# The first strip's last two groups by seven products, with the weight sums kept in the activations' places

## The chip, the cores and the metric

The program runs on one core of one Trainium2 chip. The metric is the time of one execution on the device in microseconds, measured several times; shown are the median and the extremes. The profile comes from a further execution under the hardware profiler. In its lines PE is TensorE, DVE is VectorE, ACT is ScalarE, POOL is GpSimd and SP is the engine that issues the transfers; L264 is line 264 of the kernel.

## The reference

```python
def _attn_ref(q, k, v, g_norm):                      # 8 batches, 8 heads, 576 tokens, 64 features
    kv = np.einsum('bhsd,bhse->bhde', k, v)
    out = np.einsum('bhsd,bhde->bhse', q, kv)
    rms = np.sqrt(np.mean(out * out, axis=-1, keepdims=True) + 1e-06)
    return (out / rms * g_norm).astype(np.float32)

def _moe_ref(x, w_in, w_out):                        # 4608 tokens, d_model 512, d_ff 2048
    h = x @ w_in
    r = np.maximum(h, 0.0)
    return (r * r @ w_out).astype(np.float32)
```

Linear attention without a mask, a norm per head, and a feed-forward block with squared Relu. Everything is in float32, but the two weight matrices come as 64-bit floats.

## The kernel before, in words

**Strips.** The 4608 tokens go in nine strips of 512. For each, `X @ W_in` (the first product, "up"), the squared Relu and the second product ("down") with `W_out` follow each other. Attention for the next strips is cut into slices that are put between the steps of a strip.

**Seven products for eight.** A matrix product whose operands are cut in four blocks can be made from seven block products and some sums (Strassen's scheme in Winograd's form). The kernel does so almost everywhere. For up, a group `g` (four in all) holds 256 features of each half of d_ff. `w_in` has its four blocks a11, a21, a12, a22 and `w_s` the three sums s1 = a21 + a22, s2 = s1 - a11 and s4 = a12 - s2; the last difference, a11 - a21, is written over a21. X needs four such sums too, t1 to t4. `up(s, g, p)` makes product p of a group in the order 1, 2, 6, 5, 7, 3, 4, with four matrix instructions of 128x256 each. Products 1, 6, 7 and 4 add up in one bank of PSUM ("ps_A"), 5 and 3 in another ("ps_B"), 2 in a third. `combine` takes them out: after 1, 6 and 5 ACT copies the bank to a "snap"; after 2, 7 and 3 VectorE adds the bank and a snap into a quarter of the activations `gt`; after 4 ACT takes the bank itself. A product that goes on in a bank waits until what stood in it has been taken. The snaps have the pool "c", six buffers.

**The first strip is different.** Its up is plain: `up_first` makes 128 features of 512 tokens by four instructions of 128x512, 16 steps in all, and ACT makes Relu (L915) and Square (L917). W_in's seven-product sums are not needed there; `sums_in` (L313) makes them during the first strip's down, after scaling `w_in` by the norm's weights. At that time `w_s` still holds parts of W_out in its first use.

**Weights.** They are read as 512 KB pieces of 64-bit words, two to a pair: pairs 0 to 7 are W_in (pairs 4 and 5 group 2, 6 and 7 group 3), 8 to 15 W_out. Five buffers ("raw") hold pairs on their way. A 64-bit float becomes a 32-bit one in five steps on two temporaries, w_c (two buffers) and the raw words themselves:

- L259, ACT: w_c = the upper words as float, scaled
- L261, ACT: the lower words, scaled, as integer
- L281, GpSimd: w_c limited from both sides
- L283, VectorE: w_c shifted, with the lower words' bits
- L287, VectorE: the sign put in, to `w_in`, `w_s` or `wt`

Before the last three steps of pair n are issued, `convert_pair` (L291) issues the first two of pair n+1:

```python
        for i in range(acted[0], min(n + 2, len(sources) // 2)):
            convert_pair_on_act(i)
            acted[0] = i + 1
        deque(conversion(pair_words.pop(n), dest, nc.gpsimd), 0)
        load_more(2 * n + 2)
```

`load_more` then issues the next pieces, up to ten ahead. For pairs 12 to 15 `sums_out` (L326) adds four sums on VectorE and sends what it made to DRAM, from where the blocks of W_out are streamed for down.

**Order.** The schedule is written by hand: each engine runs its instructions in the order in which the program issues them, and semaphores carry the dependences. `convert(n)` issues conversions up to number n. In the first strip's up, it is called after steps 0 to 3, before steps 4 to 9 and after steps 11 to 15. Slices of attention for batch 1 (transposed queries `t_ps`, keys and values `kv_ps`) stand between the last steps of the first up and in the down.

Of the kernel before, what the change touches and what calls it, by code (L numbers as in the profile page):

```python
# [10 lines left out]
FP32 = mybir.dt.float32  # L11
# [3 lines left out]
AF = mybir.ActivationFunctionType  # L15
ALU = mybir.AluOpType
# [4 lines left out]
def kernel(  # L21
# [54 lines left out]
    SQ = 32  # L76
    Q_ON_PE = 2
    BEHIND = 1.6
    X_ON_PE = 2
    EPS = 1e-6  # L80
    AHEAD = 10
    const = ctx.enter_context(tc.tile_pool(name="const", bufs=1))
    wpool = ctx.enter_context(tc.tile_pool(name="wpool", bufs=1))
    qkv_pool = ctx.enter_context(tc.tile_pool(name="qkv", bufs=2))
# [171 lines left out]
    def act_words(c, view, parts=(0, 1)):  # L256
        low, high_f, r = view(U32)[..., 0], view(FP32)[..., 1], view(I32)[..., 0]
        if 0 in parts:
            nc.scalar.activation(c, high_f, AF.Copy, scale=EXPONENT)  # L259
        if 1 in parts:  # L260
            nc.scalar.activation(r, low, AF.Copy, scale=TOP_THREE)  # L261

# [8 lines left out]
    def convert_pair_on_act(n):  # L271
        view = lambda dt: raw_pairs[n].bitcast(dt).rearrange("p a b (n two) -> p a (b n) two", two=2)
        c = wtmp.tile([P, 2, WN], FP32, name="w_c", tag="w_c")
        act_words(c, view)
        pair_words[n] = c, view(I32)[..., 0], view(I32)[..., 1]

    def conversion(of, dest, eng=nc.vector):
# [31 lines left out]
    def pieces_in(i):  # L309
        g, k = divmod(i // 2, KH)  # L310
        convert_pair(i // 2, w_in[:, k, g].rearrange("p (a b) e -> p a (b e)", a=2))

    def sums_in(g):  # L313

        nc.scalar.activation(w_in[:, :, g, 0:4], w_in[:, :, g, 0:4], AF.Copy, scale=g_col)
        a11, a21, a12, a22, s1, s2, s4 = (block(b)[:, :, g] for b in range(7))
        nc.vector.tensor_tensor(out=s1, in0=a21, in1=a22, op=ALU.add)
        minus(nc.vector, s2, s1, a11)
        minus(nc.vector, s4, a12, s2)
        minus(nc.vector, a21, a11, a21)  # L320
# [369 lines left out]
        return xt[s][:, ts(th, TH // SQ), ts(kh, KH), :]  # L690

    def sums_x(s):
        xc[s] = t1, t2, t3, t4 = [
            sum_pool.tile([P, TH // SQ, KH, SQ], FP32, name=f"x_t{i}", tag="sum") for i in range(4)
        ]
        x = lambda kh, th: halves(s, kh, th)
        minus(nc.vector, t1, x(0, 1), x(0, 0))
        minus(nc.vector, t2, x(1, 1), t1)
        minus(nc.vector, t3, x(1, 1), x(0, 1))
        minus(nc.vector, t4, x(1, 0), t2)  # L700
# [165 lines left out]
    def product(p, i, lhsT, rhs, n):  # L866

        for k in range(n):
            nc.tensor.matmul(  # L869
                bank[BANK[p]][:, i, :], lhsT=lhsT(k), rhs=rhs(k),  # L870
                start=p in (1, 5, 2) and i == 0 and k == 0, stop=k == n - 1, skip_group_check=True,
            )
# [46 lines left out]
    def up(s, g, p):  # L919
        open_bank(p)  # L920
        rhs = {
            1: halves(s, 0, 0), 2: halves(s, 1, 0), 3: halves(s, 1, 1),
            4: xc[s][3], 5: xc[s][0], 6: xc[s][1], 7: xc[s][2],
        }[p]
        for i in range(2):
            product(p, i, lambda kc: block(A_IN[p])[:, kc, g, ts(i, P)], lambda kc: rhs[:, :, kc, :], KH)
        dest = quarters(s, g)

        def relu_squared(q):
            def f(b, a):  # L930
                o = dest[q]
                nc.vector.tensor_tensor(out=o, in0=b, in1=a, op=ALU.add)
                nc.vector.scalar_tensor_tensor(out=o, in0=o, scalar=0.0, in1=o, op0=ALU.max, op1=ALU.mult)
            return f

        def last(b):
            nc.scalar.activation(dest[21], b, AF.Relu)
            nc.scalar.activation(dest[21], dest[21], AF.Square)

        combine(p, relu_squared(11), relu_squared(12), last, relu_squared(22))  # L940
# [417 lines left out]
    for s in range(N_STRIP):  # L1358
# [24 lines left out]
        total, done = sum(w for w, _, _ in steps), 0  # L1383
        for i, (w, fn, a) in enumerate(steps):
            if s == 0 and i < n_up:

                if 4 <= i < 10:
# [10 lines left out]
                if i == 14:  # L1398
                    for b in range(2):
                        store_first(b)  # L1400
            elif s == 0 and i == n_up:
# [9 lines left out]
                for g in range(2 * (i - n_up) - 4, 2 * (i - n_up) - 2):  # L1411
                    sum_g3(0, g)
            fn(*a)
            if s == 0 and i < 4:

                convert(3 + i)
            done += w
            if s:
                clock[0] += 3.2 if i >= n_up else 2.2 if s == DEEP else 1.2
# [42 lines left out]
            n = i + 1 - (n_up - 6)  # L1462
            pairs, m = divmod(max(n - 2 * NP, 0), 3)
            attend(min(ready[0] + min(max(n, 0), 2 * NP) + (n >= 2 * NP) + 4 * pairs + (0, 2, 2)[m], goal))
            while deep_due and i not in (n_up + 1, n_up + 4, n_up + 12, n_up + 13):
# [5 lines left out]
                    load_next(names="kv")  # L1471
            if i == n_up + 6:
                load_rest(2, nc.sync)
            if 11 <= i < n_up:

                convert((13, 13, 14, 15, 16)[i - 11])


# [28 lines left out]
```

## Time and profile before

| | us |
|---|---|
| median of 3 runs | 871.56 |
| lowest, highest | 871.21, 872.57 |
| profiled execution, its own time | 870.42 |
| its span, first to last instruction | 868.6 |
| TensorE's second product of the first strip begins (in the span) | 84.21 |

Busy time of each engine in four stretches from the span's start, in us:

| stretch | PE | DVE | ACT | POOL |
|---|---|---|---|---|
| 24 to 49 | 24.98 | 16.14 | 19.96 | 7.27 |
| 49 to 63 | 11.20 | 8.54 | 10.41 | 3.31 |
| 63 to 84 | 21.00 | 17.78 | 20.66 | 5.76 |

The granted TensorE clock is 1.00 in all of them. In a row of the timeline stand the start in us from the span's beginning, the duration, engine, line and operation, output and inputs, shape and count; the bracket, where there is one, has the engine's idle time just before and what ended it. "pair n" below always means a pair of weight pieces.

### The profile page before, as it was taken

Reading aid. Unit: us, or ns where it says so; the run is one execution under the profiler, and the core shown is the slowest. Engines: PE = TensorE matmul, PEld = TensorE weight load, DVE = VectorE, ACT = ScalarE, POOL = GpSimd, SP = SyncE. Lnnn points to the kernel's source line nnn. Section 1 sums busy time; section 2 is a strip of 40 time slices with the busy share of each in tenths; the row PEclk is TensorE's granted clock in tenths of the full one; section 3 lists DMA queues with packets and bytes.
Section 4 is the critical chain, followed back from the end, with each engine's and each line's share of the span. In section 5 each row is a group of like instructions: output and inputs, shape, how many; then the busy total and the mean of one; then the engine's idle time right before and its main releaser. Section 6 shows DMA issues by size and latency. Waiting matters only on the chain.

```text
span 868.6 us, 32423 instructions
## 1 busy us (share of the span) xinstructions
PE 858.6 (99%) x14176; PEld 804.6 (93%) x14176; DVE 700.6 (81%) x1132; ACT 349.6 (40%) x777; POOL 328.9 (38%) x335
## 2 busy tenths in 40 slices
PE   9989999999999999999999999999999999999998
PEld 7435888889999999999999999999999999999998
DVE  4668988879877996789689967897889777875887
ACT  5789251320048303740356034901491148102810
POOL 1232004530458224730574045704470447145700
PEclk9999999999999999999999999999999999999999
DMA  9997898999998996889797979997668856885483
GB/s 314 307 359 248 273 383 229 281 315 374 284 276 235 355 325 232 216 315 322 221 244 273 342 235 255 299 304 270 210 223 300 298 167 220 294 284 194 174 317 120
DMA packets 169469, 236.46 MB, mean 272 GB/s; under 512 B 78704, under 2 KB 133744, under 8 KB 161008
## 3 DMA queue, kind: packets, MB, share of 16 engines
q1 hardware_dynamic: 169024, 234.33, 83.3%
q8 instruction: 111, 1.82, 0.9%
q14 instruction: 30, 0.25, 0.1%
q10 hardware_dynamic: 304, 0.07, 0.0%
HBM read 197.66 MB, written 36.70 MB: 270 GB/s over the span
## 4 chain that ended last, share of the span: by engine, by line
PE 88%; DMA 7%; ACT 2%; SPq 2%; issue 0%; DVE 0%; ACTq 0%
PE ps_A L864 35%; PE ps_B L864 31%; PE ps_A L869 6%; PE ps_C L864 5%; PE ps_B L869 3%; DMA raw<-in_moe_w_in_dram 2%; PE x_ps L483 2%; PE kv_ps L447 2%; PE ps_C L869 2%; PE ps_A L910 1%; DMA raw<-in_moe_w_out_dram 1%; DMA w_blk<-w_deep 1%; DMA xT<-x_d 1%; DMA x_d<-x_q 1%; PE ps_C L910 1%; DMA first_qkv<-in_v_dram 1%
## 5 line engine op out<-in xcount | busy, mean ns | idle before, releaser
L864 PE MATMUL ps_B<-w_blk,g_s 128*64 128x128 f32 x2016 | 122.1, 273 | 0.0
L864 PEld LDWEIGHTS ps_B<-w_blk,g_s 128*64 128x64 f32 x2016 | 112.6, 137 | 0.1
L305 POOL TENSOR_TENSOR x_l<-xT 128x256 f32<-128x256 f32 x21 | 16.2, 770 | 230.4 <-PE ps_A L864 230.4
L864 PE MATMUL ps_B<-w_blk,gt 128*64 128x128 f32 x1504 | 94.1, 273 | 1.5 <-DMA w_blk<-w_deep 1.5
L864 PE MATMUL ps_A<-w_blk,g_s 128*64 128x128 f32 x1536 | 92.2, 273 | 0.0
L1322 POOL TENSOR_TENSOR snap<-snap,gt 128x512 f32<-128x512 f32 x35 | 46.2, 1321 | 112.3 <-ACT snap L1327 93.4
L864 PEld LDWEIGHTS ps_B<-w_blk,gt 128*64 128x64 f32 x1504 | 84.6, 137 | 2.0 <-issue 2.0
L864 PEld LDWEIGHTS ps_A<-w_blk,g_s 128*64 128x64 f32 x1536 | 85.7, 137 | 0.0
L1327 ACT COPY snap<-ps_A 128x512 f32<-128x512 f32 x63 | 36.9, 585 | 104.3 <-PE ps_A L864 96.9
L1262 ACT ACTIVATE gt<-gt 128x512 f32<-128x512 f32 x112 | 70.1, 626 | 10.5 <-DVE gt L1322 10.5
L1263 ACT ACTIVATE gt<-gt 128x512 f32<-128x512 f32 x112 | 70.7, 631 | 3.6
L864 PE MATMUL ps_A<-w_blk,gt 128*64 128x128 f32 x1152 | 71.3, 273 | 0.0
L864 PEld LDWEIGHTS ps_A<-w_blk,gt 128*64 128x64 f32 x1152 | 64.7, 137 | 0.0
L1111 ACT COPY o_sb<-ps_A 128x128 f32<-128x128 f32 x24 | 6.4, 266 | 144.9 <-PE ps_A L864 121.3
L305 DVE TENSOR_TENSOR gt<-gt 128x2048 f32<-128x2048 f32 (+1 forms) x29 | 59.7, 2063 | 0.0
L1110 DVE TENSOR_TENSOR o_sb<-o_sb,ps_B 128x256 f32<-128x256 f32 (+1 forms) x123 | 47.4, 386 | 14.6 <-ACT o_sb L1111 9.5
L1322 POOL TENSOR_TENSOR gt<-gt,snap 128x512 f32<-128x512 f32 x42 | 52.6, 1279 | 15.9 <-DVE snap L1322 15.9
L864 PE MATMUL ps_A<-x_l,w_in 128*64 128x128 f32 x896 | 58.5, 273 | 0.0
L864 PE MATMUL ps_B<-x_l,w_blk 128*64 128x128 f32 x784 | 51.3, 273 | 0.0
L864 PE MATMUL ps_A<-x_l,w_blk 128*64 128x128 f32 x784 | 51.2, 273 | 0.0
L864 PEld LDWEIGHTS ps_A<-x_l,w_in 128*64 128x64 f32 x896 | 50.8, 137 | 0.1
L1111 ACT COPY o_sb<-ps_B 128x128 f32<-128x128 f32 x31 | 8.2, 266 | 96.2 <-PE ps_B L864 96.2
(214 smaller groups left out, 1900.5 us busy)
## 6 DMA issues: line engine op xcount, KB each, us to landing
w_blk<-w_deep SPq DMA_DIRECT2D x56, 1024.0 KB, 7.3
w_blk<-w_out SPq DMA_DIRECT2D x56, 768.0 KB, 6.5
w_blk<-w_in_deep SPq DMA_DIRECT2D x49, 768.0 KB, 6.2
raw<-in_moe_w_in_dram SPq DMA_DIRECT2D x16, 512.0 KB, 8.6
raw<-in_moe_w_out_dram SPq DMA_DIRECT2D x16, 512.0 KB, 8.1
k<-in_k_dram SPq DMA_DIRECT2D x29, 256.0 KB, 5.2
v<-in_v_dram SPq DMA_DIRECT2D x29, 256.0 KB, 5.6
x_d<-x_q SPq DMA_DIRECT2D x27, 256.0 KB, 5.3
```

The lines of the kernel that those rows point to most:

```text
L305: eng.tensor_tensor(out=out, in0=a, in1=b, op=ALU.subtract)
L447: nc.tensor.matmul(ps[ts(h, D), i], lhsT=a, rhs=w, start=i == 0 and c == 0, stop=c == C, skip_group_check=True)
L483: nc.tensor.matmul(ps[half, r, i, ts(p, D)], lhsT=q[row, half], rhs=kvd[b, p][row, row], start=True, stop=True)
L864: nc.tensor.matmul(ps[half], lhsT=lhsT[:, half], rhs=rhs, start=start, stop=stop, skip_group_check=True)
L869: nc.tensor.matmul(bank[BANK[p]][:, i, :], lhsT=lhsT(k), rhs=rhs(k), start=p in (1, 5, 2) and i == 0 and k == 0, stop=k == n - 1, skip_gro ...
L910: nc.tensor.matmul(ps, lhsT=w_in[:, kc % KH, g, kc // KH * 2 + fh, ts(i, P)], rhs=xt[0][:, :, kc, :], start=kc == 0, stop=kc == NP - 1,)
L1110: add = lambda out, a, b: nc.vector.tensor_tensor(out=out, in0=a, in1=b, op=ALU.add)
L1111: yield nc.scalar.copy(q[:, 3:4], small(1))
L1262: nc.scalar.activation(o, o, AF.Relu)
L1263: nc.scalar.activation(o, o, AF.Square)
L1322: add = lambda eng, out, a, b: eng.tensor_tensor(out=out, in0=a, in1=b, op=ALU.add)
L1327: nc.scalar.copy(t, ps)
```

## The change

- Groups 2 and 3 of the first strip's up are made by `up`, seven products each, so that 8 of the 16 plain steps become 14 products.
- `first_sums_in(g)` makes s1, s2 and s4 of such a group on VectorE from unscaled weights and puts them into the places of the activations q22, q12 and q21 of the same group, which are still free; it writes a11 - a21 over a21. `sums_in` for these groups later has three sums instead of four, since a21 is already the difference.
- The first strip gets X's four sums (`sums_x(0)`), in the pool "c".
- In the first strip the Relu and Square of the quarters made by VectorE's addition go to ACT.
- The first step of the conversion moves from ACT to GpSimd (`parts` 2), with the upper limit in the same instruction.
- The times of the conversions follow a table, PACE, of 16 turns; a turn is one of the eight plain steps or 14/8 products.

```diff
+    PLAIN = 2
...
+    PACE = (3, 4, 4, 5, 6, 7, 8, 9, 10, 11, 12, 13, 13, 14, 15, 16)
...
         if 0 in parts:
             nc.scalar.activation(c, high_f, AF.Copy, scale=EXPONENT)
+        if 2 in parts:
+            nc.gpsimd.tensor_scalar(out=c, in0=high_f, scalar1=EXPONENT, scalar2=MOST, op0=ALU.mult, op1=ALU.min)
         if 1 in parts:
             nc.scalar.activation(r, low, AF.Copy, scale=TOP_THREE)
...
-        act_words(c, view)
+        act_words(c, view, (2, 1))
...
+    first_w = {}
+
+    def first_sums_in(g):
+
+        a11, a21, a12, a22 = (block(b)[:, :, g] for b in range(4))
+        dest = quarters(0, g)
+        s1, s2, s4 = first_w[g] = [dest[q] for q in (22, 12, 21)]
+        nc.vector.tensor_tensor(out=s1, in0=a21, in1=a22, op=ALU.add)
+        minus(nc.vector, s2, s1, a11)
+        minus(nc.vector, s4, a12, s2)
+        minus(nc.vector, a21, a11, a21)
...
+        if g >= PLAIN:
+            minus(nc.vector, s2, a22, a21)
+            nc.vector.tensor_tensor(out=s1, in0=s2, in1=a11, op=ALU.add)
+            minus(nc.vector, s4, a12, s2)
+            return
...
+        pool, tag = (sum_pool, "sum") if s else (c_pool, "c")
         xc[s] = t1, t2, t3, t4 = [
-            sum_pool.tile([P, TH // SQ, KH, SQ], FP32, name=f"x_t{i}", tag="sum") for i in range(4)
+            pool.tile([P, TH // SQ, KH, SQ], FP32, name=f"x_t{i}", tag=tag) for i in range(4)
...
+            b = A_IN[p]
+            w = first_w[g][b - 4] if s == 0 and b > 3 else block(b)[:, :, g]
+            product(p, i, lambda kc: w[:, kc, ts(i, P)], lambda kc: rhs[:, :, kc, :], KH)
...
                 nc.vector.tensor_tensor(out=o, in0=b, in1=a, op=ALU.add)
+                if s == 0:
+                    nc.scalar.activation(o, o, AF.Relu)
+                    nc.scalar.activation(o, o, AF.Square)
+                    return
...
-            steps = [(2, up_first, (g, fh, i)) for g in range(NG) for fh in range(2) for i in range(2)]
+            steps = [(2, up_first, (g, fh, i)) for g in range(PLAIN) for fh in range(2) for i in range(2)]
+            steps += [(1, up, (s, g, p)) for g in range(PLAIN, NG) for p in ORDER]
...
+        plain, turns = 4 * PLAIN, 4 * NG
...
+                before, at = at, i if i < plain else plain + (i - plain) * (turns - plain) // (n_up - plain)
...
             fn(*a)
-            if s == 0 and i < 4:
-
-                convert(3 + i)
+            if s == 0 and i < n_up:
+
+                if i == plain - 3:
+                    sums_x(0)
+                if i == plain - 2:
+                    first_sums_in(PLAIN)
+                if at > before:
+                    convert(PACE[at])
+                if i == plain + 3:
+                    first_sums_in(PLAIN + 1)
```

The conversions that stood before steps 4 to 9 and at the end of steps 11 to 15 are gone; the slices of attention keep their places by turns.

More of the change, by code (lines that the diff above doesn't have):

```diff
@@ L925, in up @@
         for i in range(2):
-            product(p, i, lambda kc: block(A_IN[p])[:, kc, g, ts(i, P)], lambda kc: rhs[:, :, kc, :], KH)
+            b = A_IN[p]
+            w = first_w[g][b - 4] if s == 0 and b > 3 else block(b)[:, :, g]
+            product(p, i, lambda kc: w[:, kc, ts(i, P)], lambda kc: rhs[:, :, kc, :], KH)
         dest = quarters(s, g)
@@ L1382 @@
                 goal = min(pair_ends, key=lambda end: abs(end - goal))
-        total, done = sum(w for w, _, _ in steps), 0
+        total, done, at = sum(w for w, _, _ in steps), 0, -1
+        plain, turns = 4 * PLAIN, 4 * NG
         for i, (w, fn, a) in enumerate(steps):
-            if s == 0 and i < n_up:
-                if 4 <= i < 10:
-                    convert(3 + i)
+            if s == 0:
+                before, at = at, i if i < plain else plain + (i - plain) * (turns - plain) // (n_up - plain)
+                if i >= n_up:
+                    at = turns + i - n_up
+            if s == 0 and at < turns and at > before:
                 if i == 0:
@@ L1397 @@
                         load_q_rest(b, nc.sync)
-                if i == 14:
+                if at == 14:
                     for b in range(2):
@@ L1413 @@
             fn(*a)
-            if s == 0 and i < 4:
-                convert(3 + i)
+            if s == 0 and i < n_up:
[7 more added lines that the diff above has]
+                    first_sums_in(PLAIN + 1)
             done += w
@@ L1461 @@
                 sums_x(1)
-            n = i + 1 - (n_up - 6)
+            n = at + 1 - (turns - 6)
             pairs, m = divmod(max(n - 2 * NP, 0), 3)
@@ L1473 @@
                 load_rest(2, nc.sync)
-            if 11 <= i < n_up:
-                convert((13, 13, 14, 15, 16)[i - 11])
 _INS = ['q', 'k', 'v', 'g_norm', 'moe_w_in', 'moe_w_out']
```

## The prediction

> **What bounds the kernel now.** I read first the busy shares of the whole span, then the instructions of TensorE in order of time, then those of the three engines that make its operands, between 24 and 100 us, where the change lies.
>
> ```profile
> PE 858.6 (99%) x14176; PEld 804.6 (93%) x14176; DVE 700.6 (81%) x1132; ACT 349.6 (40%) x777; POOL 328.9 (38%) x335
> ```
>
> TensorE leaves 10.0 of 868.6 us idle, so work taken from it is time won, as long as its operands are there. Time that it loses early is not won back later. TensorE in the first strip:
>
> ```profile
> 49.30 3.70 PE L910 MATMUL ps_A<-xT,w_in 128*128 128x512 f32 x8
> 55.42 3.70 PE L910 MATMUL ps_B<-xT,w_in 128*128 128x512 f32 x8 [2.42 <-ACT gt L917]
> 59.51 3.70 PE L910 MATMUL ps_A<-xT,w_in 128*128 128x512 f32 x8 [0.38 <-ACT gt L917]
> ...
> 79.95 3.60 PE L910 MATMUL ps_C<-xT,w_in 128*128 128x512 f32 x8
> ...
> 84.21 3.72 PE L869 MATMUL ps_A<-w_s,gt 128*128 128x256 f32 x16
> ```
>
> A row is one of the 16 steps, four matrix products. The waits of 2.42 and 0.38 us end with ACT, which had itself stood behind a landing:
>
> ```profile
> 39.72 1.13 ACT L259 ACTIVATE w_c<-raw 128x1024 f32<-128x1024 f32 x1 [1.73 <-DMA raw<-in_moe_w_in_dram]
> ...
> 56.09 1.15 ACT L259 ACTIVATE w_c<-raw 128x1024 f32<-128x1024 f32 x1 [0.72 <-DMA raw<-in_moe_w_out_dram]
> ```
>
> From 63 us on TensorE has no gap up to 84.21, where the second product begins. That start is my mark. VectorE and GpSimd, which turn the raw weights, pair by pair, into operands:
>
> ```profile
> 61.81 1.23 DVE L283 SCALAR_TENSOR_TENSOR w_c<-w_c,raw 128x1024 int32<-128x1024 int32 x1 [0.93 <-POOL w_c L281]
> 63.08 1.23 DVE L287 SCALAR_TENSOR_TENSOR w_s<-raw,w_c 128x1024 int32<-128x1024 int32 x1
> 65.23 1.23 DVE L283 SCALAR_TENSOR_TENSOR w_c<-w_c,raw 128x1024 int32<-128x1024 int32 x1 [0.93 <-POOL w_c L281]
> ...
> 78.65 0.68 DVE L305 TENSOR_TENSOR wt<-wt 128x512 f32<-128x512 f32 x1
> 79.25 1.54 DVE L305 TENSOR_TENSOR wt<-w_s,wt 128x512 f32<-128x512 f32 x1
> ```
>
> ```profile
> 47.10 1.93 POOL L281 TENSOR_SCALAR w_c<-w_c 128x1024 f32<-128x1024 f32 x1 [1.49 <-ACT w_c L259]
> 53.23 1.04 POOL L281 TENSOR_SCALAR w_c<-w_c 128x1024 f32<-128x1024 f32 x1 [4.20 <-ACT w_c L259]
> ...
> 79.20 1.05 POOL L281 TENSOR_SCALAR w_c<-w_c 128x1024 f32<-128x1024 f32 x1 [4.44 <-ACT w_c L259]
> ```
>
> A conversion costs VectorE 2.49 us (63.08 - 61.81, and 1.22 more), and a new one starts each 3.42 us (65.23 - 61.81). The same rows show the two engines in each other's way. GpSimd's 1.04 us took 1.93 where it began at 47.10 under a VectorE instruction that ran to 48.13, and VectorE's 0.68 took 1.54 at 79.25, where GpSimd had begun at 79.20. Each time the later one is done about its own length after the end of the earlier one: they took turns.
>
> **The change, part by part.**
>
> *Products.* Eight steps of 3.45 us (the chain of waits has 3.44 and 3.45 for L910) become 14 of 1.73 (its rows of eight L869 instructions): 27.6 - 24.2, **-3.4 us** on TensorE. The two waits before, 2.8 us, fall on steps that go, so they are counted anew below.
>
> *Conversion.* L259 moves from ACT to GpSimd for 14 pairs; ACT is relieved of some 1.05 us each and gains 2 us per group (three copies of 0.6 us, and Relu and Square on whole quarters). That shortens nothing if VectorE is later than ACT. On GpSimd I take 1.04 us, the row of the same engine, shape and kind (two operations with constants). It now reads every second word, which no GpSimd row shows; VectorE's L283 and L287 read so and cost no more per element than its sums (1.22 for 1024, 0.61 from start to start for 512), so I stay at 1.04. Lower bound 0.87: its step for 512 elements took 615 ns, so 427 ns for 512 more, with nothing for the start. Upper bound 2.1: the skipped words cost as much as the others. Near the row because a stride cost VectorE nothing.
>
> The order is what costs. The program puts the first step of pair n+1 on GpSimd ahead of the limiting step of pair n (the loop in convert_pair). There are two w_c buffers, so the step of n+1 waits until VectorE is done with pair n-1. VectorE's pair n then waits for two GpSimd instructions that could not start before its pair n-1 ended. They no longer overlap: a pair takes 2.49 + 2 x 1.04 + two handovers of 0.05, **4.67 us instead of 3.42**.
>
> *Sums.* VectorE gets 4 sums of X and 4 of W_in for each of two groups, each 0.655 us in a row of four (71.17 to 73.79). Before, the W_in sums stood in the second product, under TensorE's work. While VectorE does four sums GpSimd does its two conversion steps, and by the turns above both are paid: 2.62 + 2.08 us.
>
> *New waits.* Products 6, 7 and 4 go on in the bank of product 1. So 6 waits for ACT's copy, 7 for the next copy, 4 for VectorE's addition at 7. ACT's second copy stands behind Relu and Square of the addition at 2, and that addition stands on VectorE behind the conversions of pairs 8 and 9. Queued behind these on TensorE are the transposes and keys of batch 1 and everything later. SP's order changes little: the last raw pair and four stores go ahead of the keys of (1,3), and the stores of w_out come later with VectorE. The stream of w_out blocks follows them; it was issued at 100.11 and used from 110.07, so it moves with TensorE.
>
> *The sum, along VectorE.* Pair 5 lands at 39.6 as before (ACT's row). GpSimd: its step to 40.8, the limit of pair 4 to 41.8; VectorE's pair 4 to 44.3; two GpSimd steps; pair 5 starts at **46.5** (45.64 was pair 6 before). From there to the addition at 7 of the last group, which releases TensorE's last product, VectorE and GpSimd do in turn:
> - nine conversions, pairs 5 to 13: 9 x 2.49 = 22.4
> - 20 sums (X, two groups of W_in, two of W_out): 20 x 0.655 = 13.1
> - five additions from PSUM, 0.65 each (L932 took 0.69): 3.2, of which two lie beside GpSimd, -1.3
> - GpSimd's two steps after each of the nine, and a third after the last: 19 x 1.04 = 19.8
>
> 46.5 + 57.2 = 103.7. The last product takes 1.73 and the keys after it 0.73 (chain of waits): the second product starts at **106.2 instead of 84.21, +22 us**. A check on TensorE's side: product 7 of the third group starts when pairs 8 and 9 (two turns of 4.67 after pair 7 ends at 63.3), the addition (0.6), Relu, Square and the copy (three times 0.6) are through, near 75; product 5 ended near 62. That one wait is 13 us; the others (6 and 4 of this group, 6, 7 and 4 of the next) are 2 to 4 us each. Together some 27.5, less the 2.8 of before and the 3.4 of products: +21.3.
>
> Behind the mark VectorE loses two of its eight W_in sums (1.2 us), under TensorE's work: nothing, unless its later start leaves it late once more; 0 to +2, I take +1. **Sum: 870.42 + 23 = 893.4 for a profiled run**; that run stood 1.1 under the median of 871.56, so the median is **894.5**.
>
> **The rivals.**
> 1. *Faster: TensorE stays the bound.* If conversions keep their 3.42 us and the sums fit into VectorE's waits, the 3.4 us are won, and the 2.8 of ACT's waits too, as ACT loses its L259: 865 to 868 us. For it: ACT is 20.66 of 21 us busy from 63 to 84, GpSimd only 5.76. Against: the two w_c buffers and GpSimd's order. It decides from a turn of 3.5 us or less, and the rows add up to 4.67.
> 2. *Only the turn of the buffers, no exclusion.* GpSimd then works under the sums: five times 2.08 us and once 1.04 come off the sum, -11.4: 883. Against it: 1.93 and 1.54 us above.
> 3. *GpSimd reads every second word slowly.* At 2.1 us, ten to twelve steps on the path cost 1.06 more: +11 to +13, 905 to 908. Against it stands VectorE's stride.
> 4. *TensorE comes back slowly from the 13 us gap.* At the start of the span 14 rows of L391 take 3.29 us for seven 128x128 products, 0.47 each, where L910 has 0.86 for four times the columns, 0.215: 1.8 us lost at one start. After 2.42 us of idle time at 55.42 the next step took its usual 3.70. If the gap is long enough, products of 1.73 take up to 3.5 until TensorE is steady again. Most of that lies under VectorE's lateness of 2 to 4 us per wait; what does not is the last product and the first of the second product: +1.8 to +4, 896 to 899.
>
> On this a rule of the Trainium skill speaks, in "TensorE: Matmul & The Clock Gate", Part 1: after some 3.4 us without work the array falls to half its clock, and needs as long of steady work to rise. By that rule rival 4 is what happens; the trace of before can't tell, with no later gap over 2.42 us and a granted clock of 1.00 in every slice.
>
> **How the numbers follow.** My case 0.50 (891 to 898, with GpSimd's steps at 1.0 to 1.2); rival 1 0.05; rival 2 0.16; rival 3 0.12; rival 4 0.14; what lies between these 0.03, of which 0.01 would be no change. The range runs from rival 2 with the lower price of GpSimd's step, 881, to rival 3 at 907. What a measurement tells from no change is 0.2%, 1.7 us, and only rival 1 comes out faster: faster 0.05, no change 0.01, slower 0.94.
>
> **What would show it.** In the changed profile: VectorE's pairs 8, 9 and 10 start 4.7 us apart, each wait ended by GpSimd; the two GpSimd instructions before each are 1.04 us alone and 1.6 beside sums; one TensorE wait of about 13 us near 62 to 75, ended by ACT; L869 reads w_s first at 106. I am wrong if the pairs start 3.5 us apart, if sums beside GpSimd keep 0.68, if GpSimd's new row is over 1.3, or if the time after the mark is not that of before within 2 us.

## The result, and the profile after

The changed kernel takes 918.3 us (917.76 to 921.21) against 871.87 (871.21 to 872.57) beside it: 1.054 times as long, 95% interval 1.0514 to 1.0565. Foretold were 894.5 us and a range of 881 to 907. The direction and the turn of the buffers were as foretold; the price of one instruction was not, and with it about half of the loss. The profiled execution took 921.21 us, its span is 919.3.

First the busy line and the group of the new instruction, from the page of the changed kernel (line numbers are now those of the changed kernel: GpSimd's new step is L263, its limiting step, called clamp below, L285, VectorE's two steps L287 and L291, the differences L309, the copies to a snap L901, the additions L956):

```profile
PE 866.6 (94%) x14224; PEld 819.2 (89%) x14224; DVE 717.7 (78%) x1148; ACT 337.6 (37%) x761; POOL 379.9 (41%) x349
...
L263 POOL TENSOR_SCALAR w_c<-raw 128x1024 f32<-128x1024 f32 x14 | 53.7, 3836 | 33.0 <-DVE w_in L291 14.7
```

TensorE's idle time rose from 10.0 to 52.7 us (919.3 - 866.6). The second line holds the suspect: GpSimd's new instruction takes 3.84 us in the mean, where the forecast has 1.04. The two engines in order of time, VectorE first:

```profile
42.90 1.23 DVE L287 SCALAR_TENSOR_TENSOR w_c<-w_c,raw 128x1024 int32<-128x1024 int32 x1 [4.92 <-POOL w_c L285]
50.29 1.22 DVE L287 SCALAR_TENSOR_TENSOR w_c<-w_c,raw 128x1024 int32<-128x1024 int32 x1 [4.91 <-POOL w_c L285]
...
68.61 1.45 DVE L309 TENSOR_TENSOR gt<-gt,w_in 128x512 f32<-128x512 f32 x1
70.10 0.69 DVE L309 TENSOR_TENSOR gt<-w_in,gt 128x512 f32<-128x512 f32 x1
70.71 0.68 DVE L309 TENSOR_TENSOR w_in<-w_in 128x512 f32<-128x512 f32 x1
```

```profile
45.47 3.67 POOL L263 TENSOR_SCALAR w_c<-raw 128x1024 f32<-128x1024 f32 x1 [2.60 <-DVE w_in L291]
49.22 1.04 POOL L285 TENSOR_SCALAR w_c<-w_c 128x1024 f32<-128x1024 f32 x1
...
68.06 4.05 POOL L263 TENSOR_SCALAR w_c<-raw 128x1024 f32<-128x1024 f32 x1 [2.60 <-DVE w_in L291]
```

Read the turn (from the start of one pair on VectorE to that of the next) as a ring. VectorE starts at 42.90; its two steps end at 45.4; only then GpSimd starts the first step of the next pair but one (45.47), then the limit (49.22), and at 50.29 VectorE may go on. 7.39 us per pair, nothing beside anything else, and both waits are ended by the engine that the prediction names. The rows from 68.61 show something else: while GpSimd's 4.05 us ran (68.06 to 72.11), one of VectorE's three sums was lengthened, the other two took their usual 0.69 and 0.68. TensorE:

```profile
45.44 4.48 PE L932 MATMUL ps_A<-xT,w_in 128*128 128x512 f32 x6 [6.22 <-DVE w_in L291]
...
70.21 3.75 PE L891 MATMUL ps_A<-x_t,gt 128*128 128x256 f32 x8 [6.53 <-DVE gt L309]
92.98 3.75 PE L891 MATMUL ps_A<-x_t,w_in 128*128 128x256 f32 x8 [16.18 <-ACT snap L901]
102.01 2.47 PE L891 MATMUL ps_A<-x_t,w_in 128*128 128x256 f32 x8 [3.12 <-DVE gt L956]
...
127.79 3.72 PE L891 MATMUL ps_A<-w_s,gt 128*128 128x256 f32 x16
```

The second product begins at 127.79 instead of 84.21, 43.6 us later; nearly the whole loss of 46.4 us is there before that mark. The first row shows a wait that the prediction does not have: already in the plain steps TensorE waits 6.22 us for W_in, because the early pairs are late as well.

### The profile page after: what moved, and what is told of

Read it like the earlier page. It is cut to its first block, busy times and chain, and to the rows that moved or that the text cites. A ratio compares the mean times of both kernels' runs of the same rounds, so it can differ in the third digit from the quotient of the medians.

```text
span 919.3 us, 32563 instructions
## 1 busy us (share of the span) xinstructions
PE 866.6 (94%) x14224; PEld 819.2 (89%) x14224; DVE 717.7 (78%) x1148; ACT 337.6 (37%) x761; POOL 379.9 (41%) x349
## 4 chain that ended last, share of the span: by engine, by line
PE 83%; POOL 7%; issue 4%; DMA 2%; ACT 2%; DVE 2%; SPq 0%; POOLq 0%; DVEq 0%
PE ps_A L886 34%; PE ps_B L886 30%; PE ps_A L891 5%; POOL w_c L263 5%; PE ps_C L886 5%; PE ps_B L891 3%; PE x_ps L504 2%; PE kv_ps L468 2%; POOL w_c L285 2%; PE ps_C L891 2%; DMA first_qkv<-in_v_dram 1%; DVE w_c L287 1%; DMA q_rest<-in_q_dram 1%; DMA v<-in_v_dram 0%; ACT x_n L606 0%
## 5 line engine op out<-in xcount | busy, mean ns | idle before, releaser
L886 PE MATMUL ps_B<-w_blk,g_s 128*64 128x128 f32 x2016 | 121.8, 273 | 0.0
L886 PEld LDWEIGHTS ps_B<-w_blk,g_s 128*64 128x64 f32 x2016 | 112.4, 137 | 0.1
L309 POOL TENSOR_TENSOR x_l<-xT 128x256 f32<-128x256 f32 x21 | 16.5, 788 | 229.7 <-PE ps_A L886 229.7
L886 PE MATMUL ps_B<-w_blk,gt 128*64 128x128 f32 x1504 | 94.0, 273 | 0.0
L886 PE MATMUL ps_A<-w_blk,g_s 128*64 128x128 f32 x1536 | 92.0, 273 | 0.0
L886 PEld LDWEIGHTS ps_A<-w_blk,g_s 128*64 128x64 f32 x1536 | 85.5, 137 | 0.0
L886 PEld LDWEIGHTS ps_B<-w_blk,gt 128*64 128x64 f32 x1504 | 84.6, 137 | 0.3 <-issue 0.3
L886 PE MATMUL ps_A<-w_blk,gt 128*64 128x128 f32 x1152 | 71.0, 273 | 0.0
L263 POOL TENSOR_SCALAR w_c<-raw 128x1024 f32<-128x1024 f32 x14 | 53.7, 3836 | 33.0 <-DVE w_in L291 14.7
L886 PEld LDWEIGHTS ps_A<-w_blk,gt 128*64 128x64 f32 x1152 | 64.5, 137 | 0.0
L309 DVE TENSOR_TENSOR gt<-gt 128x2048 f32<-128x2048 f32 (+1 forms) x29 | 59.7, 2063 | 0.0
L886 PE MATMUL ps_A<-x_l,w_in 128*64 128x128 f32 x896 | 59.3, 273 | 0.2 <-DVE gt L1350 0.2
L287 DVE SCALAR_TENSOR_TENSOR w_c<-w_c,raw 128x1024 int32<-128x1024 int32 (+1 forms) x18 | 20.7, 1149 | 46.1 <-POOL w_c L285 41.2
L886 PE MATMUL ps_A<-x_l,w_blk 128*64 128x128 f32 x784 | 52.2, 273 | 2.5 <-issue 2.5
L886 PE MATMUL ps_B<-x_l,w_blk 128*64 128x128 f32 x784 | 52.0, 273 | 1.4 <-issue 1.4
```

Source lines behind the costliest of these rows:

```text
L263: nc.gpsimd.tensor_scalar(out=c, in0=high_f, scalar1=EXPONENT, scalar2=MOST, op0=ALU.mult, op1=ALU.min)
L287: yield nc.vector.scalar_tensor_tensor(out=ci, in0=ci, scalar=3, in1=r, op0=ALU.logical_shift_left, op1=ALU.bitwise_or)
L309: eng.tensor_tensor(out=out, in0=a, in1=b, op=ALU.subtract)
L886: nc.tensor.matmul(ps[half], lhsT=lhsT[:, half], rhs=rhs, start=start, stop=stop, skip_group_check=True)
```

## The experiments

Each kernel is compared with runs of the kernel before on the same chip (medians from 870.22 to 872.69 us). "Mark" is the start of the second product in the one profiled execution; the two profiles of the changed kernel differ by 1.0 us in it. All results in one table; the sections below tell what each was for.

| kernel | GpSimd's first step | mark, us | time, us | ratio to before | 95% interval |
|---|---|---|---|---|---|
| before | none (ScalarE) | 84.21 | 871.87 | 1 | |
| changed | multiply, min | 127.79 | 918.3 | 1.054 | 1.0514 to 1.0565 |
| changed, once more | multiply, min | 126.76 | 913.84 | 1.0496 | 1.0443 to 1.0548 |
| changed, operations exchanged | min, max | 128.45 | 916.96 | 1.0529 | 1.0472 to 1.0587 |
| changed, limit first | multiply, min | 106.27 | 893.43 | 1.0267 | 1.0220 to 1.0314 |
| changed, two multiplications | multiply, multiply | 104.34 | 895.88 | 1.0272 | 1.0247 to 1.0297 |
| the same, limit first | multiply, multiply | 98.98 | 889.02 | 1.0196 | 1.0173 to 1.0220 |
| changed, step on ScalarE | none | 92.71 | 880.4 | 1.0112 | 1.0076 to 1.0149 |
| before, step on GpSimd | multiply, min | 100.40 | 910.93 | 1.0455 | 1.0410 to 1.0500 |
| before, two multiplications | multiply, multiply | 83.46 | 882.96 | 1.0140 | 1.0112 to 1.0169 |
| the same, limit first | multiply, multiply | 81.77 | 875.96 | 1.0055 | 1.0033 to 1.0078 |

### Is it the step, or the sums and products?

The changed kernel with the step back on ScalarE:

```diff
-        act_words(c, view, (2, 1))
+        act_words(c, view)
```

> The changed kernel with the first step of the conversion (L263) back on ScalarE; products, sums and order of the conversions as changed. Theory A (GpSimd's 3.84 us for that step, twice in the turn with the clamp, carries nearly all of the loss): pairs start some 3.4 us apart again, VectorE does nine pairs at 3.42 and 20 sums at 0.655, part of them in its 0.93 us waits, the second product starts at 86 to 92, time 873 to 881. Theory B (the sums, the seven products and their new waits on copies and additions cost as much as the step): second product after 100, time over 888.

Measured: mark 92.71, 880.4 us. That is Theory A, at the upper end of its time and 0.7 us beyond that of its mark. The other half of the test, the kernel before with nothing but this step moved:

```diff
+        if 2 in parts:
+            nc.gpsimd.tensor_scalar(out=c, in0=high_f, scalar1=EXPONENT, scalar2=MOST, op0=ALU.mult, op1=ALU.min)
...
-        act_words(c, view)
+        act_words(c, view, (2, 1))
```

> The kernel before with nothing changed but the first step of the conversion, moved from ScalarE to GpSimd as in the change; no new sums, no seven products in the first strip. Theory A: pairs start 7.4 us apart, eleven pairs (5 to 15) lose 4.0 us each, of which TensorE feels what W_in's and W_out's last pairs bring: 900 to 918. Theory B: under 885, because TensorE's chunks for the first strip need no copies and additions between them.

Measured: 910.93 us, mark 100.40, and in the second product one further wait of 14.1 us that VectorE ends. So the step alone costs 40.7 us, and the rest of the change alone 10.2; together they cost 46.4 (41.2 when the changed kernel was measured once more, below), less than the sum of 50.9.

### Is the turn the order of GpSimd's steps?

In this kernel GpSimd's clamp of a pair goes ahead of the first step of the next one (`conversion` gives its steps one at a time; `next` issues the first of them, the clamp):

```diff
-        for i in range(acted[0], min(n + 2, len(sources) // 2)):
-            convert_pair_on_act(i)
-            acted[0] = i + 1
-        deque(conversion(pair_words.pop(n), dest, nc.gpsimd), 0)
+        for i in range(acted[0], n + 1):
+            convert_pair_on_act(i)
+            acted[0] = i + 1
+        steps = conversion(pair_words.pop(n), dest, nc.gpsimd)
+        next(steps)
+        for i in range(acted[0], min(n + 2, len(sources) // 2)):
+            convert_pair_on_act(i)
+            acted[0] = i + 1
+        deque(steps, 0)
```

> The changed kernel, but GpSimd's clamp of pair n is issued ahead of the first step of pair n+1. Theory A1 (the turn of 7.4 us is VectorE's 2.49 and GpSimd's two steps one after the other, because the two w_c buffers and GpSimd's order forbid an overlap): now the first step of n+1 runs under VectorE's part of pair n, a turn is GpSimd's own 3.7 to 4.2 + 1.05 = 4.8 to 5.3 us, second product at 92 to 104, time 880 to 893. Theory A2 (GpSimd and VectorE exclude each other for the whole of an instruction): under VectorE's 1.23 us steps the 3.7 us step is pushed back, a turn stays over 6.5 us, time over 905.

Measured: 893.43 us, mark 106.27 instead of 126.76 and 127.79: some 21 us of the loss go with the order alone. GpSimd and VectorE in this kernel:

```profile
42.00 4.73 POOL L263 TENSOR_SCALAR w_c<-raw 128x1024 f32<-128x1024 f32 x1
46.81 1.04 POOL L285 TENSOR_SCALAR w_c<-w_c 128x1024 f32<-128x1024 f32 x1
47.93 4.72 POOL L263 TENSOR_SCALAR w_c<-raw 128x1024 f32<-128x1024 f32 x1
```

```profile
41.95 1.23 DVE L287 SCALAR_TENSOR_TENSOR w_c<-w_c,raw 128x1024 int32<-128x1024 int32 x1 [2.67 <-POOL w_c L285]
43.21 2.01 DVE L291 SCALAR_TENSOR_TENSOR w_in<-raw,w_c 128x1024 int32<-128x1024 int32 x1
```

Now VectorE works under GpSimd's step, but each pays: 4.73 instead of 3.68 and 2.01 instead of 1.23. The turn is 5.93 us, between the two theories (4.8 to 5.3, over 6.5). GpSimd has hardly any idle time left in it (0.1 us between its steps): with this order its own two steps are the bound.

### What makes the price?

The prediction had weighed one thing only, that the step reads every second word. In the next kernel the two GpSimd steps exchange their operations, so that the strided step limits and the packed one multiplies:

```diff
-            nc.gpsimd.tensor_scalar(out=c, in0=high_f, scalar1=EXPONENT, scalar2=MOST, op0=ALU.mult, op1=ALU.min)
+            nc.gpsimd.tensor_scalar(out=c, in0=high_f, scalar1=MOST / EXPONENT, scalar2=-MOST / EXPONENT, op0=ALU.min, op1=ALU.max)
...
-    def conversion(of, dest, eng=nc.vector):
+    def conversion(of, dest, eng=nc.vector, limits=(MOST, -MOST, ALU.min, ALU.max)):
...
-        yield eng.tensor_scalar(out=c, in0=c, scalar1=MOST, scalar2=-MOST, op0=ALU.min, op1=ALU.max)
+        yield eng.tensor_scalar(out=c, in0=c, scalar1=limits[0], scalar2=limits[1], op0=limits[2], op1=limits[3])
...
-        deque(conversion(pair_words.pop(n), dest, nc.gpsimd), 0)
+        deque(conversion(pair_words.pop(n), dest, nc.gpsimd, (EXPONENT, MOST, ALU.mult, ALU.min)), 0)
```

> The changed kernel with the operations of GpSimd's two steps exchanged: the step that reads every second word limits from both sides (min, max, with limits 2^112 times larger), and the step on packed words multiplies and takes the minimum. Theory S (the 8-byte step between the words read costs it): L263 stays at 3.7 us, L285 at 1.04. Theory M (a multiplication costs it): L263 falls to 1.04, L285 rises to 3.7. The time stays near 918 under S and under M.

The groups of GpSimd between 24 and 130 us (busy time, mean in ns):

```profile
L285 POOL TENSOR_SCALAR w_c<-w_c 128x1024 f32<-128x1024 f32 x14 | 53.5, 3819 | 1.1
L263 POOL TENSOR_SCALAR w_c<-raw 128x1024 f32<-128x1024 f32 x14 | 17.7, 1261 | 35.5 <-DVE w_in L291 19.9 <-DVE w_s L291 10.4 <-DVE wt L291 5.2
```

The price went with the operations: the packed step has 3.82 us, the one that reads every second word 1.26 in the mean. The stride costs next to nothing, Theory S falls. Which operations? A list, one extra instruction for each pair, in the kernel before:

```diff
+    def probe(n, c):
+        if n == 2:
+            nc.gpsimd.tensor_scalar(out=c, in0=c, scalar1=1.0, scalar2=None, op0=ALU.mult)
...
+        if n == 14:
+            nc.gpsimd.tensor_scalar(out=c, in0=c, scalar1=2.0, scalar2=0.5, op0=ALU.mult, op1=ALU.mult)
...
+        probe(n, pair_words[n][0])
         deque(conversion(pair_words.pop(n), dest, nc.gpsimd), 0)
```

> The kernel before with one more GpSimd instruction on w_c (128x1024, packed words, in place, without effect on the values) ahead of the clamp of pairs 2 to 14, another operation for each. Theory M1 (any multiplication or addition is slow on GpSimd, limits and copies are not): multiply alone, add alone, and each pair of operations with one of them take 2 us and more, min alone, min with max and max with min 1.05 or less, and the sum of two tensors, whose rows in the kernel before are 1.3 us for 512 elements, 2.6 us. Theory M2 (only a pair that mixes arithmetic with a limit is slow): multiply alone, multiply with multiply and add alone take 1.05, multiply with min and add with min 3.7. Theory M3 (each multiplication adds 2.7 us): multiply 3.7, multiply with multiply 6.4.

None of the three held. Multiply with multiply took 2.09 and 1.75 us beside VectorE, far less than multiply alone (2.79 and 3.63) and add alone (3.52); a minimum alone took 2.77, min with max 1.78 beside VectorE, but max with min 4.38; a copy took 1.04, and the sum of two tensors 1.89, not the 2.6 of Theory M1. As VectorE lengthens such rows, the list was made again with the extra instruction where VectorE waits (the kernel before with two multiplications, below):

> The kernel before with the conversion's first step on GpSimd by two multiplications, and for pairs 3 to 12 one more GpSimd instruction on w_c (128x1024, packed, without effect on the values) between this step and the clamp, where VectorE waits for GpSimd and does nothing. Theory P (two operations of one kind for which rows near 1.04 were seen, multiply-multiply and min-max, are fast, and all else, single operations too, takes a slower way): multiply, add and min alone 2.7 us, multiply-multiply and min-max 1.04, max-min, multiply-min, min-multiply, add-add and multiply-add 3.6. Theory Q (VectorE beside them made the single ones slow): multiply, add and min alone 1.04, and only mixed pairs 3.6.

GpSimd's rows, in the order multiply; add; min; multiply, multiply; min, max; max, min; multiply, min; multiply, add:

```profile
38.11 2.81 POOL L295 TENSOR_SCALAR w_c<-w_c 128x1024 f32<-128x1024 f32 x1
...
45.72 2.78 POOL L297 TENSOR_SCALAR w_c<-w_c 128x1024 f32<-128x1024 f32 x1
...
53.40 2.77 POOL L299 TENSOR_SCALAR w_c<-w_c 128x1024 f32<-128x1024 f32 x1
...
60.98 1.04 POOL L301 TENSOR_SCALAR w_c<-w_c 128x1024 f32<-128x1024 f32 x1
...
66.92 1.04 POOL L303 TENSOR_SCALAR w_c<-w_c 128x1024 f32<-128x1024 f32 x1
...
72.88 3.63 POOL L305 TENSOR_SCALAR w_c<-w_c 128x1024 f32<-128x1024 f32 x1
...
81.42 3.63 POOL L307 TENSOR_SCALAR w_c<-w_c 128x1024 f32<-128x1024 f32 x1
...
106.98 1.04 POOL L313 TENSOR_SCALAR w_c<-w_c 128x1024 f32<-128x1024 f32 x1
```

Theory P, with one exception: multiply-add is fast as well. Three pairs run at 1.04 us (multiply-multiply, min-max, multiply-add), any other pair of this list takes 3.63 to 3.75 (min with multiply 3.64, add with add 3.75), a single operation 2.8. Two more pairs of the first list, add with min (3.63) and max with multiply (4.67), are slow too. Even the order of min and max decides: 1.04 or 3.63. The instruction's shape and type are the same in all rows. Why the engine is slow for some operations and not for others, no run shows.

### The same change at the foretold price

As two multiplications are fast and the limit that follows takes the minimum anyway, the foretold price can be had with one argument pair:

```diff
-            nc.gpsimd.tensor_scalar(out=c, in0=high_f, scalar1=EXPONENT, scalar2=MOST, op0=ALU.mult, op1=ALU.min)
+            nc.gpsimd.tensor_scalar(out=c, in0=high_f, scalar1=EXPONENT, scalar2=1.0, op0=ALU.mult, op1=ALU.mult)
```

> The changed kernel with one argument pair changed: L263 multiplies by the same factor and then by 1.0 (instead of taking the minimum; the clamp that follows takes it anyway). Two multiplications were among the pairs of operations that the price list showed near 1.04 us without a neighbour (2.09 and 1.75 beside VectorE). If the pair of operations is the whole price, L263 falls from 3.84 to 1.04 to 1.6 us. Then this run tests the rest of the prediction: by its sum (VectorE and GpSimd strictly in turn, 4.67 us per pair) the second product starts at 106 and the time is 893 to 895; if GpSimd's steps run under the sums in part, as its 3.7 us did in the changed kernel, 95 to 102 and 881 to 889. If the skipped words do cost a multiplication something, L263 stays at 2 us or more and the time over 896.

Measured: 895.88 us (894.5 was foretold for a price of 1.04). VectorE, GpSimd and TensorE of this kernel:

```profile
41.69 1.23 DVE L287 SCALAR_TENSOR_TENSOR w_c<-w_c,raw 128x1024 int32<-128x1024 int32 x1 [2.36 <-POOL w_c L285]
...
46.51 1.23 DVE L287 SCALAR_TENSOR_TENSOR w_c<-w_c,raw 128x1024 int32<-128x1024 int32 x1 [2.34 <-POOL w_c L285]
```

```profile
44.25 1.10 POOL L263 TENSOR_SCALAR w_c<-raw 128x1024 f32<-128x1024 f32 x1 [2.60 <-DVE w_in L291]
45.44 1.04 POOL L285 TENSOR_SCALAR w_c<-w_c 128x1024 f32<-128x1024 f32 x1
```

```profile
74.20 3.78 PE L891 MATMUL ps_A<-x_t,w_in 128*128 128x256 f32 x8 [12.68 <-ACT snap L901]
...
101.69 1.99 PE L891 MATMUL ps_A<-x_t,w_in 128*128 128x256 f32 x8 [0.48 <-DVE gt L956]
104.34 3.72 PE L891 MATMUL ps_A<-w_s,gt 128*128 128x256 f32 x16
```

The step takes 1.10 us, strided as it is. The turn is 4.82 us (4.67 foretold), pair 5 starts at 46.51 (46.5), the long wait is 12.68 and ended by ScalarE (13, by ScalarE), the mark is 104.34 (106.2). So at the foretold price the turn, the long wait and the time come out near what was foretold. The small waits do not: the other five of the two groups take 0.4 to 1.9 us (2 to 4 foretold). Between this run and the changed kernel lie 22.4 and 23.5 us at the mark (126.76 and 127.79 less 104.34), from 2.6 us on one instruction (3.68 and 1.10 alone).

The limit first (the diff shown for it above), with this price:

> As the run with two multiplications, and with GpSimd's clamp of pair n issued ahead of the first step of pair n+1. Theory: the turn is then no longer VectorE's 2.49 plus two GpSimd steps; by full exclusion it saves nothing but the handovers (second product 104, 891), without exclusion the second product starts at 85 and the time is 871. The rows of 1.5 to 2.0 us of sums and conversions beside GpSimd's clamp speak for nearer the first: 95 to 104, 881 to 891.

889.02 us, mark 98.98: 5.4 us of the mark are won by the order, where the slow step had given some 21. Now both engines' instructions are lengthened where they meet: GpSimd's two steps take some 2.1 and 1.9 us and VectorE's second one 2.02, so that most of what the order could bring is lost again.

The kernel before with the same two multiplications on GpSimd, without seven products and sums, in both orders:

> The kernel before with the conversion's first step on GpSimd by two multiplications; no seven products and no new sums in the first strip. The turn by the prediction is 4.67 us. W_in's pairs end earlier than TensorE needs them, W_out's pairs 12 to 15 end some 8 to 12 us later than before. If TensorE's stream of W_out blocks feels that: 880 to 887, with waits at ps_B for g_s or for w_blk behind the second product's start, which itself stays within 83 to 88. If the turn does not matter: 868 to 872, as ScalarE's waits for landings (2.8 us on TensorE) go.

> As the kernel before with two multiplications on GpSimd, and with the clamp of pair n issued ahead of the first step of pair n+1. If the order of GpSimd's steps is what lengthens the turn: 3.4 to 3.8 us per pair, 866 to 871. If GpSimd's and VectorE's exclusion lengthens it: over 4.3 us per pair, 877 to 885.

The first gives 882.96 us with the mark at 83.46, and the loss lies behind it, as the first expectation has it: a wait of 4.9 us at ps_B for g_s, ended by VectorE. The second gives 875.96; its turn is 4.2 us (42.39, 46.60, 50.82 on VectorE), between the two expectations. It is the nearest that any kernel with this step came, and still slower than before. TensorE's waits for ScalarE in the first product are gone in it (mark 81.77), but VectorE's 3.42 us per pair are not reached; the loss lies behind the mark, where the longest wait, 2.6 us, is for a block of W_out.

### What is left without GpSimd's step

The 10 us that remain with the step on ScalarE were looked into by three edits of that kernel. One group instead of two by seven products:

```diff
-    PLAIN = 2
+    PLAIN = 3
...
-                if i == plain + 3:
-                    first_sums_in(PLAIN + 1)
```

> The changed kernel with L263's step on ScalarE, and only the last of the four groups by seven products (PLAIN = 3); the other twelve steps plain. Theory V (with the step on ScalarE it is VectorE's work that is late, 0.655 us per sum and addition): four first sums and three additions fewer, 4.6 us less work on VectorE, of which GpSimd's turns and loads leave some 3: second product at 88 to 91, time 875 to 879. Theory W (the waits of products 6, 7 and 4 for a bank of PSUM carry the loss): half of the 10.2 us of waits goes and half of the 3.4 us won on products with it: 876 to 877, but the first addition stands as late in its group as before, with a wait of some 7 us.

Relu and Square of the added quarters back on VectorE:

```diff
-                if s == 0:
-                    nc.scalar.activation(o, o, AF.Relu)
-                    nc.scalar.activation(o, o, AF.Square)
-                    return
```

> The changed kernel with L263's step on ScalarE, and Relu and Square of the six quarters made by VectorE's additions back on VectorE, in one instruction of 0.65 to 0.7 us each. Theory V: VectorE gets 6 x 0.655 = 3.9 us more; second product at 95 to 97, time 883 to 885. Theory W: ScalarE's copies come earlier, as Relu and Square (1.2 us for each quarter) no longer stand ahead of them: second product at 90 to 92, time 877 to 880.

The sums of X twice in the first strip:

```diff
-        minus(nc.vector, t1, x(0, 1), x(0, 0))
...
+        for _ in range(1 if s else 2):
+            minus(nc.vector, t1, x(0, 1), x(0, 0))
...
```

> The changed kernel with L263's step on ScalarE, and the four sums of X made twice, with the same result. Theory V: 4 x 0.655 = 2.6 us more VectorE work ahead of the last addition, 2.0 to 3.5 us later with GpSimd's turns: second product at 94.7 to 96.2, time 882.5 to 884. Theory W: the sums lie in a stretch where TensorE still has plain steps; the second product stays at 92.7, time 880.

| step on ScalarE, and | mark, us | time, us | ratio | 95% interval |
|---|---|---|---|---|
| nothing more | 92.71 | 880.4 | 1.0112 | 1.0076 to 1.0149 |
| one group | 89.07 | 880.13 | 1.0101 | 1.0082 to 1.0121 |
| Relu and Square on VectorE | 94.33 | 885.33 | 1.0173 | 1.0132 to 1.0213 |
| X sums twice | 93.57 | 882.65 | 1.0139 | 1.0118 to 1.0160 |

More VectorE work goes with a later mark, less with an earlier one, as Theory V has it, but not by its full size: with 2.6 us more of sums the mark is 0.9 later, with 3.9 us of Relu and Square 1.6. These are single profiles, marks of one kernel differ by 1.0, and the intervals of the ratios overlap: the direction fits Theory V, its size is not shown. Where the longest wait comes from is seen on ScalarE in the kernel with nothing more, and on TensorE beside it:

```profile
51.81 1.16 ACT L261 ACTIVATE w_c<-raw 128x1024 f32<-128x1024 f32 x1 [1.92 <-DMA raw<-in_moe_w_out_dram]
...
57.30 1.15 ACT L261 ACTIVATE w_c<-raw 128x1024 f32<-128x1024 f32 x1 [2.13 <-DVE w_in L291]
58.34 1.18 ACT L265 ACTIVATE raw<-raw 128x1024 int32<-128x1024 uint32 x1
59.38 0.60 ACT L901 COPY snap<-ps_A 128x512 f32<-128x512 f32 x1
```

```profile
49.34 1.89 PE L891 MATMUL ps_A<-xT,w_in 128*128 128x256 f32 x8
51.06 1.89 PE L891 MATMUL ps_C<-xT,w_in 128*128 128x256 f32 x8
60.04 3.78 PE L891 MATMUL ps_A<-x_t,gt 128*128 128x256 f32 x8 [7.09 <-ACT snap L901]
```

Product 1 had ended by 51.3, but its copy (59.38) stands in ScalarE's order behind the first steps of two more pairs: the first of them waited 1.92 us for a landing, the second 2.13 us for VectorE. So theories V and W are in part one chain: VectorE's lateness, and a landing, reach TensorE through a copy that has nothing to do with weights. A third cause is seen later in the same profile: from 80.18 on TensorE has no gap up to the mark, and there, after a wait of 2.43 us, a product took 3.11 us instead of 1.99 and the keys behind it took 0.5 us longer than usual. By these rows some 1.6 of the 8.5 us at the mark are TensorE's slow return, an estimate.

The median with one group (880.13) lies above the 875 to 879 of Theory V, although its mark (89.07) is where that theory has it. The mark belongs to the fastest of its four executions, 877.74 us, which lies in the range; the other three took 880.1 to 880.7, and why is open.

### The changed kernel once more

> The changed kernel as it is, once more. The second product starts at 127 to 129 again, and the span behind it is 785 to 789 (before: 784.4; two multiplications: 787.5), so that its time is 914 to 919; if the 791.5 of the first profile belong to the change, 791 again and 918 to 922.

913.84 us; the span behind the mark is 785.9 (912.7 - 126.76), against 791.5 in the first profile and 784.4 before. In the first profile TensorE's waits on L886 put down to "issue" come to 6.8 us, in this one to 2.3. The first profile is of the slowest of its four executions. The 7 us are thus mostly a difference between executions; some 1.5 us stay in the second profile, within what was foretold.

## Why the prediction was wrong, by its own steps

*The price of GpSimd's step: the step that failed.* "I take 1.04 us, the row of the same engine, shape and kind (two operations with constants)", with 2.1 us as upper bound. Measured: 3.67 to 3.69 alone, 3.84 in the mean. The fault is the word "kind": the row was of min with max, the new instruction is multiply with min, and on this engine these are not one kind (1.04 and 3.63). The bound was then drawn from the stride, the one property that turned out to cost nothing (1.10 us strided, 1.04 packed). The trace of before held a warning, in rows that were not consulted for the bound: GpSimd's additions and differences of two tensors took 1.28 to 1.32 us for 512 elements, 2.5 ns each, where the clamp has 1.0. From them the upper bound would have been 2.6 us (3.3 from the dearest group of that size, 1.67 us in the mean), still too low, but the choice of 1.04 would have had to be defended against it. The text had named the row that would prove this step wrong, one over 1.3. Three of its four signs of being wrong came: this row, sums that keep 0.68 beside GpSimd (most of them do beside the slow step), and in the first profile the time after the mark.

On this point the Trainium skill, "GPSIMD Engine Reference", section 4.1 (Engine selection), says that GpSimd runs elementwise operations with one input at roughly line rate. The rows agree for three pairs of operations and a copy (1.04 us for 1024 elements, one per nanosecond) and disagree for all others tried (2.8 to 3.75).

*The turn of the buffers: right.* Two GpSimd steps between two turns of VectorE; 4.82 us at the foretold price, 7.39 at the real one, which is 2.49 + 3.67 + 1.04 and handovers.

*The exclusion: nearly right at the foretold price, wrong at the real one.* At 1.10 us a turn with four sums in it took 6.59 us (46.51 to 53.10) against 4.82: 1.8 of the 2.6 us charged were paid. Beside the slow step, the four sums from 67.89 on lengthened a turn by 0.4 us (65.49 to 73.26 is 7.77, against 7.39). The stretch from pair 5 to pair 14 shows it as a whole: nine turns with 20 sums and five additions in them. In the changed kernel it takes 68.8 us (57.70 to 126.47), 2.3 more than nine bare turns of 7.39; with two multiplications 55.0 us (46.51 to 101.55), 11.7 more than nine of 4.82, where the prediction charged 15.0. So rival 3, whose 1.06 us per step for "ten to twelve steps" grows to 28 to 34 us at the real price, would have led to 922 to 928, above what came: it adds the price on top of sums that in truth run under it. The sum, in turn, starts the path at pair 5, but a dearer step is paid on the pairs before it too: of the 23.5 us between the two kernels at the mark 11.2 are there when pair 5 starts (57.70 and 46.51).

On this the Trainium skill, "SBUF — State Buffer", section "Who interferes with whom", calls the ports that VectorE and GpSimd share an exclusive lock, and says that a VectorE instruction with two inputs contends for them with a GpSimd instruction that reads. The 1.04 us steps beside sums fit (1.4 to 1.5 us instead of 0.7). The 4.05 us step fits no lock that lasts for a whole instruction: sums of 0.69 and 0.68 us ran to their end inside it.

*The near hit at the foretold price* (mark 104.34, foretold 106.2) is partly luck: the sum counts 4.57 us for a turn, which takes 4.82, some 2 us too little over nine turns, and 3.3 us too much for sums and additions.

*The sums and products: not foretold apart.* Without any step on GpSimd the rest of the change cost 10 us. The prediction has no such case, so its terms for them (13.1 us of VectorE work, 3.4 us won on products) are tested only within the whole.

*TensorE's slow return (rival 4): it happens, and in the changed kernel it is hidden.* The product (eight rows of the trace) after a long gap took 3.75 us instead of 1.99 (3.78 with two multiplications), and the granted clock of the changed kernel between 63 and 106 us is 0.65 to 0.66 (0.72 to 0.73 in its second profile). In both kernels none of VectorE's additions before the mark waited for TensorE, and the last product took its usual 1.99, so nothing of it reached the mark. It is not hidden with the step on ScalarE (some 1.6 us, above). The length of the last gap does not decide alone: 1.96 us came before a step of 3.50 in the second profile of the changed kernel, and two later gaps of 1.99 and 1.96 us there before steps of 1.99; 2.42 us before a plain step cost nothing in the kernel before.

*Behind the mark: about right.* +1 was foretold; the second profile has 1.5, the first 7.1, and the run with two multiplications 3.1 (787.5 against 784.4).

Of the 43 us at the mark, 22 to 23.5 are the price of the pair of operations (changed against two multiplications), 11.6 the step's presence on GpSimd at 1.1 us (two multiplications against the step on ScalarE), and 8.5 the sums, products and copies, with TensorE's slow return in them. The shares hold in this order only: without the new sums and products the step at 1.1 us does not move the mark (83.46 against 84.21), so the 11.6 us are paid only where both meet.

## What to carry to other kernels

Price an instruction by a row with the same operations, not only with the same engine, shape and type; where there is none, take the engine's dearest row per element as the upper bound (here even that, by rows of 512 elements, was below the 3.67 us measured), and weigh each property that differs, not only the one that looks odd. An instruction that sits in a ring of two buffers and two engines costs its price once per turn: here 2.6 us too much became 22. And where an operation is free to choose (a factor of 1.0 for a minimum that is taken later anyway), try the pair that has been seen to be fast.

## What was not expected of the hardware

GpSimd's two-operation instruction on 128x1024 float words took 1.04 us for multiply-multiply, multiply-add and min-max, 3.63 for max-min and multiply-min, and 2.8 for a single multiplication, addition or minimum: one operation costs more than some pairs of two. Beside a slow form some of VectorE's two-input instructions keep their usual time (0.69 and 0.68 us within a step of 4.05); beside two of 1024 elements one after the other the slow form grew from 3.68 to 4.73 us.
